# Converting the raw words of a weight piece before its place is free

## The chip, the core and the metric

The kernel runs on one core of a Trainium2 chip. Its engines are TensorE (matmuls into PSUM), VectorE, ScalarE, GpSimd and SyncE (SP, which issues most of the transfers); each works through a queue of its own in order. The metric is the device time of one execution in microseconds, the median over runs. The times vary by about 0.1% from run to run.

## What is computed

Attention over 4 batches of 8 heads with 576 positions and 64 columns, causal by blocks of 64; then a gated layer on 2304 tokens of 512 columns; then a layer of 8 experts of which each token uses two. Cut to what matters:

```python
scores = where(mask, q @ k.T / 8, -1e9)
x = softmax(scores) @ v                      # 32 heads, then (2304, 512)
x = ((x @ w1) * (x @ w2)) @ w3 @ w_out       # w3 (1024, 1024), w_out (1024, 512)
out = sum of the two best experts' weights * (relu(x @ m1[e]) @ m2[e])
```

## The kernel before

**Precision and pieces.** Every float32 operand of a matmul is split into a high part, rounded to the matmul's type (ScalarE, L489), and a low part, the difference (VectorE or GpSimd, L493); a product is three matmuls (L498, L499, L500). The weights of the gated layer arrive as the raw 64-bit words of doubles. They are loaded piece by piece into a raw buffer (`load64`, L554, two buffers, on SP's queue), turned into float32 by three integer instructions on VectorE (`conv64`, L563, L564, L565) in one staging buffer (`stf`, there is only one), and split from there into a place: one of twelve tiles pc0 to pc11, of 2 x 1024 columns.

**The product of the weights.** While the attention of the first heads runs, the kernel also works out w3 @ w_out, once, in 64 units of three matmuls of 512 columns (`w_unit`); eight units make one half of a result tile (pc8 to pc11). w_out lies in pc0 to pc3; the eight slices of w3 pass through pc4 and pc5 in turn. Then the slices of w1 and w2 take pc6, pc7, and pc4, pc5, pc0 to pc3 once the product is done. So most pieces have a place that units still read. The list of jobs has 23 pieces (`w_jobs`), each with its source, its place and the number of units that must have been emitted before the place can be taken over (the last entry, `at`): 16 to 48 for the slices of w3 from the third on, 64 for the last six pieces, else 0.

**The order.** The program is written out as a loop over heads: the pass i emits what ends head i and what starts head i + 1, in the order of a string of steps (FIRST for the first ten passes, LATER behind them): g and s and a and b are units of the attention, `c` is a call of `feed`, `f2.9` a call of `fill`. FIRST has three of each. `feed` splits the piece that was converted in the call before, then converts the next one, if the counter of units allows it, and issues the load of the one after the next. `fill` emits units of the product as long as enough pieces are split (`moe1.conv`), for 2.9 us of matmul time by a number in the code (0.65 a unit), else nothing. When the units are used up, it emits steps of the gated layer.

**What stands in the queues.** The framework then orders each engine's queue at build, by what is ready and by the place of an instruction in the emitted program. Offsets in the code shift that place: pieces count as emitted 60 instructions later (PIECE_PRIO), units of the product 400 later (W_PRIO), the gated layer's matmuls 200 later (MOE_PRIO). So the place of a step in the program is not the time at which it runs, but once built, the order on each engine is fixed.

**Other lines that are named.** L660 and L663 are the matmuls of the scores (tile sb), L674 the reductions that find each row's maximum (negated), L677 joins the two of the last tile of a head (once in a head). L628 to L633 split q and k, L693 transposes the probabilities, L699 splits them from head 8 on, L718 multiplies by v. L196 (GpSimd) and L201 (VectorE) make the first tokens of the gated layer out of eight heads' results: a sum, and a product with the reciprocals of the row sums.

Of the kernel before, what the change touches and what calls it, by code (L numbers as in the profile page):

```python
# [476 lines left out]
class Kernel:  # L477
# [91 lines left out]
    def attention(self):  # L569
# [3 lines left out]
        with tc.tile_pool(name="p1", bufs=1, side="right") as p1, \  # L573
# [162 lines left out]
            wst = {}  # L736
# [18 lines left out]
            def w_jobs():  # L755

                def wout(g):
                    return a["w_out"][:, g:g + 1, :], 1, g // 2, (g % 2) * 512, 0

                def wout2(g):  # L760
                    return a["w_out"][:, g:g + 2, :], 2, g // 2, 0, 0

                def w3(ft, o, w=512):
                    return a["w3"][ft, :, o:o + w].unsqueeze(1), 1, 4 + ft % 2, o, 0 if ft < 2 else max(16, 8 * (ft - 1))

                for half in range(2):
                    for ft in range(2):
                        yield w3(ft, half * 512)
                    if half == 0:
                        for g in range(2):  # L770
                            yield wout(g)
                    for g in range(2 + 2 * half, 4 + 4 * half, 2):
                        yield wout2(g)
                for ft in range(2, 8):
                    yield w3(ft, 0, 1024)
                for m, (n, k, i) in enumerate(W12):
                    yield a[n][:, :, k * 256:(k + 1) * 256], 4, i, 0, 0 if m < 2 else 64

            jobs = list(w_jobs())
            raw = []  # L780

            conv = []

            def feed():

                with tc.high_priority(offset=PIECE_PRIO):
                    feed_half()

            def feed_half():
                if len(conv) > wst.get("split", 0):  # L790
                    _, _, i, o, _ = jobs[len(conv) - 1]
                    pc, w = self.pc[i], conv[-1].shape[-1]
                    self.split((pc[:, 0, o:o + w], pc[:, 1, o:o + w]), conv[-1], low="dve")
                    wst["split"] = len(conv)
                    moe1.conv += w // 512
                n = len(conv)
                if n < len(jobs) and wst.get("n", 0) >= jobs[n][4]:
                    conv.append(self.conv64(raw[n]))
                    if n + 2 < len(jobs):
                        raw.append(self.load64(*jobs[n + 2][:2]))  # L800
# [370 lines left out]
```

## Time and profile before

| | us |
|---|---|
| median of three runs | 1068.72 (1068.28 to 1069.4) |
| the profiled execution, its own time | 1066.87 |
| its span, first to last instruction | 1065.0 |
| TensorE busy in it | 1030.6 (97%) |
| VectorE, ScalarE, GpSimd busy | 558.3, 497.8, 306.5 |

The profile is one execution, 1.85 us faster than the median of the runs. Times inside it count from the start of the span. A busy TensorE is not one at its peak, since matmuls are pipelined and their ends are modelled; an idle one is a loss if it has work that waits. The heads' attention fills the first 440 us, the product of the weights lies in its first 126 us, and the experts' layer ends the kernel.

### The profile page before, as it was taken

How to read it: one execution, taken by the hardware profiler on the slowest of the kernel's cores; microseconds unless marked ns; L12 is line 12 of the kernel's file. 1: busy time of each engine (PE TensorE's matmuls, PEld its weight loads, DVE VectorE, ACT ScalarE, POOL GpSimd, SP SyncE). 2: the span in 40 equal slices, each digit the busy share in tenths (PEclk: the TensorE clock that was granted, in tenths of full speed). 3: DMA queues.
4: the chain of work that ended last, by engine and by line, in shares of the span. 5: the costliest groups of instructions: out<-in, count | busy, mean ns of one | idle time of the engine just before them, and what ended most of it. 6: DMA issues, size and time to landing. Idle time of an engine off the chain costs nothing.

```text
span 1065.0 us, 17408 instructions
## 1 busy us (share of the span) xinstructions
PE 1030.6 (97%) x6612; PEld 932.9 (88%) x6612; DVE 558.3 (52%) x1198; ACT 497.8 (47%) x1176; POOL 306.5 (29%) x309
## 2 busy tenths in 40 slices
PE   6899898999999999999999999999999999999996
PEld 4677697898999999899999889989898989899896
DVE  7987999585755757534245443533333333434110
ACT  6775567565665665523224433533333333334110
POOL 1000334234252425142345134341404132220212
PEclk9999999999999999999999999999999999999998
DMA  8764786437542553222424355763646454351312
GB/s 278 255 229 131 226 243 127 121 111 167 165 115 85 152 181 96 74 87 60 80 61 120 96 126 148 208 178 72 159 99 156 103 149 109 110 119 31 40 20 33
DMA packets 78722, 136.34 MB, mean 128 GB/s; under 512 B 21245, under 2 KB 46053, under 8 KB 77477
## 3 DMA queue, kind: packets, MB, share of 16 engines
q1 hardware_dynamic: 68149, 113.19, 36.5%
q0 software_dynamic: 10480, 21.95, 11.3%
q8 instruction: 54, 0.88, 0.4%
q14 instruction: 39, 0.32, 0.1%
HBM read 103.92 MB, written 31.19 MB: 127 GB/s over the span
## 4 chain that ended last, share of the span: by engine, by line
PE 88%; DVE 8%; ACT 1%; issue 1%; DMA 1%; POOL 0%; SPq 0%; POOLq 0%; DVEq 0%; ACTq 0%
PE ph L498 14%; PE ph L500 14%; PE ph L499 14%; PE m L498 10%; PE m L499 10%; PE m L500 10%; PE av L718 4%; PE tp L693 4%; PE sb L663 2%; PE sb L660 2%; PE m L977 2%; DVE nm L674 1%; DVE stf L564 1%; DVE stf L565 1%; DVE hi L630 1%
## 5 line engine op out<-in xcount | busy, mean ns | idle before, releaser
L498 PE MATMUL m<-xh,pc 128*128 128x256 f32 x576 | 162.2, 286 | 0.6 <-DVE lgs L285 0.3
L499 PE MATMUL m<-xh,pc 128*128 128x256 f32 x576 | 159.8, 282 | 0.0
L500 PE MATMUL m<-xh,pc 128*128 128x256 f32 x576 | 159.2, 282 | 0.0
L499 PE MATMUL ph<-xt,pc 128*128 128x384 f32 (+1 forms) x512 | 156.9, 307 | 0.0
L500 PE MATMUL ph<-xt,pc 128*128 128x384 f32 (+1 forms) x512 | 156.9, 306 | 0.0
L498 PE MATMUL ph<-xt,pc 128*128 128x384 f32 (+1 forms) x512 | 156.3, 307 | 0.0
L994 DVE SCALAR_TENSOR_TENSOR ht<-ph,ht 128x384 fp32r<-128x384 f32 (+1 forms) x128 | 62.2, 490 | 148.1 <-ACT ht L993 148.1
L493 DVE TENSOR_TENSOR pc<-stf,pc 128x1024 fp32r<-128x1024 f32 (+1 forms) x75 | 87.7, 1182 | 88.7 <-ACT pc L489 83.0
L498 PE MATMUL ph<-pc,ht 128*128 128x512 f32 (+1 forms) x328 | 127.9, 390 | 0.0
L1040 POOL DMA_INDIRECT out_dram<-yo,ids x39 | 65.4, 1677 | 213.4 <-ACT yo L1036 98.7
L499 PE MATMUL ph<-pc,ht 128*128 128x512 f32 (+1 forms) x328 | 125.9, 384 | 0.0
L500 PE MATMUL ph<-pc,ht 128*128 128x512 f32 (+1 forms) x328 | 125.9, 385 | 0.0
L993 ACT ACTIVATE ht<-ph 128x384 fp32r<-128x384 f32 (+1 forms) x128 | 55.6, 438 | 132.3 <-PE ph L500 132.0
L679 ACT ACTIVATE pb<-sb,nm 128x288 f32<-128x288 f32 (+3 forms) x192 | 93.8, 498 | 46.3 <-PE tp L693 26.9
L498 PEld LDWEIGHTS m<-xh,pc 128*128 128x128 f32 x576 | 107.9, 189 | 1.4 <-DVE ps L341 0.6
L499 PEld LDWEIGHTS m<-xh,pc 128*128 128x128 f32 x576 | 107.7, 188 | 0.6
L500 PEld LDWEIGHTS m<-xh,pc 128*128 128x128 f32 x576 | 107.1, 188 | 0.3
L493 POOL TENSOR_TENSOR gt<-at,gt 128x256 fp32r<-128x256 f32 x72 | 58.9, 821 | 146.5 <-ACT gt L489 146.3
L489 ACT CAST pc<-stf 128x1024 fp32r<-128x1024 f32 (+1 forms) x75 | 75.0, 1016 | 47.0 <-DMA stf<-in_m_dram 30.1
L499 PEld LDWEIGHTS ph<-xt,pc 128*128 128x128 f32 x512 | 96.1, 188 | 0.3
L498 PEld LDWEIGHTS ph<-xt,pc 128*128 128x128 f32 x512 | 96.1, 188 | 0.4
L500 PEld LDWEIGHTS ph<-xt,pc 128*128 128x128 f32 x512 | 96.2, 188 | 0.0
(162 smaller groups left out, 2170.7 us busy)
## 6 DMA issues: line engine op xcount, KB each, us to landing
stf<-in_m_dram SPq DMA_DIRECT2D x52, 512.0 KB
qk<-in_qk_dram SPq DMA_DIRECT2D x31, 576.0 KB
stg<-in_w_dram SPq DMA_DIRECT2D x14, 1024.0 KB
x<-ev SPq DMA_DIRECT2D x64, 144.0 KB
xab<-x SPq DMA_DIRECT2D x10, 512.0 KB
yt<-y SPq DMA_DIRECT2D x18, 260.0 KB
v<-in_v_dram SPq DMA_DIRECT2D x24, 160.0 KB
out_dram<-cst SPq DMA_DIRECT2D x3, 1280.0 KB
```

Source lines behind the costliest of these rows:

```text
L489: d = nc.scalar.copy(h, src)
L493: return d, eng.tensor_tensor(l, src, r32(h), op=OP.subtract)
L498: nc.tensor.matmul(out, a, c, start=first, stop=False)
L499: nc.tensor.matmul(out, a, d, start=False, stop=False)
L500: nc.tensor.matmul(out, b, c, start=False, stop=last)
L660: nc.tensor.matmul(o, lh, c.hi[:, 1, k0:k0 + w], start=True, stop=False)
L679: nc.scalar.activation(pb[t][:, k0:k0 + src.free_size()], src, AF.Exp, bias=nm, scale=1.0, accum_out=sums[:, h // H, t + n, h % H:h % H + 1])
L693: nc.tensor.transpose(bank[:, n * P:(n + 1) * P], pb[t][:, kt * P:(kt + 1) * P], self.ident)
L718: nc.tensor.matmul(c.av[:, o0:o0 + w], c.vv[:, kt, :], c.pt[:, i, s0:s0 + w], start=(kt == 0 and i == 0), stop=(kt == 4 and i == m - 1))
L993: a = nc.scalar.activation(hh[:, 0, f, :], ph, AF.Relu)
L994: v = nc.vector.scalar_tensor_tensor(hh[:, 1, f, :], ph, 0.0, r32(hh[:, 0, f, :]), op0=OP.max, op1=OP.subtract)
L1040: d = nc.gpsimd.indirect_dma_start(out=self.a["out"], out_offset=self.idx(e, i), in_=yo, in_offset=None, compute_op=OP.add)
```

## The change

The counter of units no longer holds back the conversion of a piece (nor the load that follows it), only its split. A call of `feed` that finds a converted piece whose place is not yet free by the counter does nothing; otherwise it splits that piece and always converts the next one.

```diff
             def feed_half():
                 if len(conv) > wst.get("split", 0):
-                    _, _, i, o, _ = jobs[len(conv) - 1]
+                    _, _, i, o, at = jobs[len(conv) - 1]
+                    if wst.get("n", 0) < at:
+                        return
                     pc, w = self.pc[i], conv[-1].shape[-1]
                     self.split((pc[:, 0, o:o + w], pc[:, 1, o:o + w]), conv[-1], low="dve")
                     wst["split"] = len(conv)
                     moe1.conv += w // 512
                 n = len(conv)
-                if n < len(jobs) and wst.get("n", 0) >= jobs[n][4]:
+                if n < len(jobs):
                     conv.append(self.conv64(raw[n]))
                     if n + 2 < len(jobs):
                         raw.append(self.load64(*jobs[n + 2][:2]))
```

## Rows read from the trace of the kernel before

**Rows 1.** Windows: stretch, length, busy us of each engine (instructions), granted clock, transfers.
```profile
76.00:107.00 31.00, 31.00 (x166) 24.57 (x165) 22.08 (x35) 18.92 (x50) 0.00 (x0) 1.00 0.45 146
126.00:138.00 12.00, 8.66 (x42) 6.70 (x41) 11.94 (x18) 7.91 (x20) 4.40 (x3) 0.72 0.67 225
138.00:166.00 28.00, 27.55 (x222) 25.99 (x221) 27.57 (x40) 19.68 (x54) 11.53 (x8) 1.00 0.79 233
166.00:181.00 15.00, 10.00 (x74) 8.80 (x74) 14.94 (x26) 10.85 (x28) 8.01 (x5) 1.00 0.37 94
181.00:1065.00 884.00, 873.46 (x5695) 804.55 (x5693) 397.93 (x947) 376.95 (x866) 270.88 (x267) 1.00 0.44 110
```

**Rows 2.** The chain of waits up to 260 us: start, length, what.
```profile
85.98 0.46 PE m L498 x2
...
176.92 1.74 DVE stf L565
```

**Rows 3.** Timeline of VectorE: start, length, line, operation, out<-in, count.
```profile
112.54 0.15 DVE L677 TENSOR_REDUCE nm<-nm 128x1 f32<-128x2 f32 x1
...
181.03 1.21 DVE L493 TENSOR_TENSOR pc<-stf,pc 128x1024 fp32r<-128x1024 f32 x1
```

**Rows 4.** Timeline of VectorE around pieces 11 and 12.
```profile
78.35 1.22 DVE L493 TENSOR_TENSOR pc<-stf,pc 128x1024 fp32r<-128x1024 f32 x1
...
80.08 0.68 DVE L563 TENSOR_SCALAR stf<-stg 128x1024 int32<-128x1024 int32 x1
...
82.33 1.22 DVE L565 SCALAR_TENSOR_TENSOR stf<-stg,stf 128x1024 int32<-128x1024 int32 x1
```

**Rows 5.** Window of L500's matmuls alone (units of the product, one each): TensorE, its weight loads.
```profile
0.00:85.00 85.00, 10.84 (x29) 5.46 (x29) 1.00 0.74 240
```

**Rows 6.** Timeline of ScalarE: high halves of pieces 12 and 14.
```profile
90.13 1.05 ACT L489 CAST pc<-stf 128x1024 fp32r<-128x1024 f32 x1
...
106.64 1.05 ACT L489 CAST pc<-stf 128x1024 fp32r<-128x1024 f32 x1 [0.97 <-PE m L499]
```

**Rows 7.** Groups on VectorE, 76 to 107 us, then one of 107 to 181.
```profile
L674 DVE TENSOR_REDUCE nm<-sb 128x1 f32<-128x288 f32 (+4 forms) x14 | 6.0, 456 | 4.6 <-PE sb L663 4.4
...
L564 DVE SCALAR_TENSOR_TENSOR stf<-stg,stf 128x1024 int32<-128x1024 int32 x3 | 3.7, 1223 | 0.1
L565 DVE SCALAR_TENSOR_TENSOR stf<-stg,stf 128x1024 int32<-128x1024 int32 x3 | 3.7, 1219 | 0.0
...
L565 DVE SCALAR_TENSOR_TENSOR stf<-stg,stf 128x1024 int32<-128x1024 int32 x8 | 11.1, 1393 | 0.1
```

**Rows 8.** Waits of SP's queue, 0 to 200 us: us in total, times, longest.
```profile
SPq L554 <- DVE stf L565: 24.7, 10, 4.5
```

**Rows 9.** Timeline of TensorE: first and last of twelve matmuls, and the product's last.
```profile
118.56 0.39 PE L498 MATMUL m<-pc,pc 128*128 128x512 f32 x1
...
121.08 0.39 PE L500 MATMUL m<-pc,pc 128*128 128x512 f32 x1
...
124.89 0.39 PE L500 MATMUL m<-pc,pc 128*128 128x512 f32 x1
```

**Rows 10.** Timeline of TensorE: the first scores of two heads.
```profile
38.33 0.25 PE L660 MATMUL sb<-hi 128*128 128x192 f32 x1
...
44.70 0.49 PE L660 MATMUL sb<-hi 128*128 128x192 f32 x1
```

**Rows 11.** Waits of VectorE, 76 to 107 us.
```profile
DVE nm L674 <- PE sb L663: 4.4, 2, 3.1
```

**Rows 12.** Timelines of GpSimd and VectorE: the first tokens.
```profile
125.61 0.92 POOL L196 TENSOR_TENSOR xab<-xab 128x256 f32<-128x256 f32 x1 [4.14 <-DMA xab<-x]
...
133.03 0.43 DVE L201 TENSOR_TENSOR xr<-xab,xr 128x256 f32<-128x256 f32 x1
```

**Rows 13.** Windows, columns as in rows 1.
```profile
126.00:129.00 3.00, 1.61 (x9) 0.94 (x7) 3.00 (x6) 2.99 (x9) 0.58 (x2) 1.00 0.71 257
...
131.00:137.00 6.00, 5.17 (x22) 4.10 (x22) 5.94 (x10) 4.08 (x11) 1.83 (x2) 0.50 0.87 284
```

## The prediction

> **What bounds the kernel now.** I read the windows of the trace by stage first, then the chain of waits, then the queues of VectorE, ScalarE, TensorE and the load queue around the weight pieces. In the windows [rows 1] the reader is to see three regimes. Until 107 us TensorE is busy without a break (31.00 of 31.00 us in 76 to 107) while VectorE has 31.00 - 22.08 = 8.92 us idle. From 126 to 181 us it is the other way round: VectorE is busy 11.94 of 12, 27.57 of 28 and 14.94 of 15 us, and TensorE loses 3.34 + 0.45 + 5.00 = 8.79 us. After 181 us TensorE has work to the end (873.46 of 884 us). The chain of waits says the same [rows 2]: it runs over matmuls of the weight product near 86 us, and over the conversion of a piece (L565) still at 177 us. So only the first 181 us can be touched by this change, and there the price of a gain is read from VectorE: what it finishes earlier than 181 us lets TensorE fill again earlier, at most the 8.79 us.
>
> **Where the pieces stand.** There are 23 pieces. I number them from 0 in the order of the list of jobs; pieces 9 to 14 are the slices of w3 that reuse two places (pc4, pc5), and 17 to 22 are slices of w1 and w2 that reuse places of the product. Counting the counters through the two order strings by hand, before and after, gives this. Before, five feed calls split a piece and convert nothing, since the next one's place is in use (after pieces 8, 10, 11, 12 and 16). After, three calls do nothing instead (ahead of the splits of 12, 13 and 17). So the conversions and splits of 9 and 10 are emitted one feed call earlier, and those of 11 to 22 two, the conversions of 12, 13 and 17 three; the last split moves from the second feed of the pass i = 7 to the third of i = 6. With three such calls to a pass (one head) that is a third of a head to a whole one.
>
> But emission is not execution. The order string puts the last split before the last scores of head 8. Those scores' minimum runs at 112.54 us and the split at 181.03 us [rows 3]: 68 us after its place in the program. The pieces trail because they share one staging buffer: a conversion needs the split before it done. Look at pieces 11 and 12 [rows 4]: the split of 11 starts at 78.35 us, and the conversion of 12 follows at 80.08 and ends at 82.33 + 1.22 = 83.55 us. Its place (pc5) is read by the units of the product up to the 32nd, and at 85 us 29 of them had run their last matmul [rows 5]; ScalarE's half of its split comes at 90.13 us [rows 6]. **So the conversion already runs while the place is in use**, 10 us before the split. For piece 14, too, what ends ScalarE's wait at 106.64 us is a matmul of the product (L499), not the conversion [rows 6]. What the change asks for is, in time, there already.
>
> **The change part by part.**
> 1. Raw conversions emitted earlier: three instructions each for 14 pieces (9 to 22), none added, none removed. They are already behind the split of the piece before; the single buffer keeps them there. 0 us. If the cover were gone (the conversion really moved by a feed), one piece is 0.68 + 1.22 + 1.22 and 1.22 us for its low half, 4.3 us of VectorE [rows 4, 7].
> 2. The early return in the feed call, which holds back the split alone: a split in time waits for the matmuls, not for the counter [rows 6]. 0 us. No wait is added on an engine, since the counter is Python's, at build time.
> 3. Raw loads, 1 MB each, issued with the conversions on SP's queue: they need one of two raw buffers, and what SP's queue waits for there is the conversion's last instruction, 24.7 us in ten waits [rows 8]. Issued earlier in the program they wait for the same. 0 us; below, at most what the loads of the next head's q and k would be held behind them.
> 4. Units of the product (L498 to L500, 64 units of three matmuls): each one from 16 on is emitted one fill call earlier, because the counter of split pieces that gates them is higher at that call. This is the one thing that can really move on TensorE. Twelve of these matmuls start from 118.56 to 121.08 us, so 0.229 us each, 0.69 a unit, 5.5 us for the eight that free a place [rows 9]. A fill emits up to five units, 3.4 us. But a unit is emitted with an offset of 400 instructions behind the attention's, so it mostly fills holes that the attention leaves, and being emitted one fill earlier changes its turn only where it competes. Lower bound: nothing moves, 0 us. Upper bound: every unit comes 3.4 us earlier. Then pieces 11 to 14 follow 3.4 us earlier, which brings 3.4 / 5.5 x 4.3 = 2.7 us of VectorE work into the idle 8.92 us; but the heads make way by 3.4 us of 6.4 (the same matmul of two heads with no unit between, 38.33 and 44.70 us [rows 10]), and with them go 3.4 / 6.4 x 2.6 = 1.4 us of their score reductions (14 reductions are 6.0 us, six to a head [rows 7]). Net -1.3 us. I take -0.5 us, nearer to nothing, since the rows show fillers.
>
> The last instruction of a conversion, L565, is dearer late: 1219 ns in 76 to 107 us, where GpSimd does nothing, and 1393 ns in 107 to 181 [rows 1, 7]. A piece that slid from the later stretch into the earlier would save 0.17 us there, too little to enter the sum. The Trainium skill's page "SBUF — State Buffer", section "Who interferes with whom", says that VectorE and GpSimd share one port pair as an exclusive lock, which speaks for moving conversions to where GpSimd is quiet; the rows agree in direction, and by the rule too the sum changes by some 0.2 us a piece.
>
> **The sum.** The profiled execution took 1066.87 us (span 1065.0 and 1.87 around it); 1066.87 - 0.5 = 1066.4. That execution is 1.85 us under the median of the runs shown (1068.72), so as a median I forecast 1068.72 - 0.5 = 1068.2 us.
>
> **The rivals.** What one of these runs can tell from no change is about 0.2%, 2.1 us.
>
> A, the forecast: the early emission meets the single staging buffer, and only a few units change their turn. 1068.2 us, own range 1066.7 to 1070.3. For it speaks the early conversion [rows 3 to 6]. Against it: every queue's order is fixed at build, so one unit taken earlier deals the order behind it anew; A needs that this comes out even.
>
> B, faster: the units win their turns, the places come free earlier, and one whole piece (4.3 us) fits into VectorE's idle time before 107 us, which is mostly waiting for score matmuls that stand behind other work in TensorE's queue (4.4 us of it [rows 11]). The crowded stretch then ends near 176.7 instead of 181 us, the loss of TensorE there falls from 8.79 to about 4.5 us, and the time is 1068.72 - 4.3 = 1064.4 us. For it: the gap is twice as long as a piece, and the pieces behind 14 are one chain. Against it: heads pushed back leave a gap of their own.
>
> C, slower: the units are used up earlier while the attention and the first tokens of the next layer come no earlier. The units are what fills TensorE until 124.89 us [rows 9]. The tokens' sum is ready at 126.5 us, and the product with the reciprocals waits in VectorE's queue until 133.03 us [rows 12], so a head 7 that is up to 6.5 us later costs nothing there, and an earlier end of the units gains nothing. TensorE is then without filler from 121.5 us. By the idle share of the hole (3.34 of 12 us [rows 1]) that is 3.4 x 0.28 = 0.95 us more. The hole also has a price in clock: TensorE was busy 1.61 of the 3 us from 126 to 129 us, and from 131 to 137 us the granted clock is 0.50, the lower level of 1.2 GHz, with 5.17 of 6 us of matmuls in it [rows 13]. 3.4 us more at half the pace with matmuls in 0.86 of it lose 1.46 us. 1068.72 + 2.4 = 1071.1 us. It decides where the last unit ends before 122 us and VectorE's crowd does not end sooner. The Trainium skill's page "TensorE: Matmul & The Clock Gate", section "What's actually happening", says that "the default state is throttled, and activity releases the throttle"; by that rule a longer hole is paid at the lower clock, and this trace agrees with its 0.50.
>
> **How the numbers follow.** A 0.46, B 0.30, C 0.24. A is likeliest since the conversions already run in front of their splits; B is above C because the idle time of VectorE that it uses is there, and C's loss partly hides behind a VectorE that is full anyway. The range for 8 in 10 reaches to both: 1064.3 to 1071.4 us. Faster by over 0.2%: 0.30; within: 0.46; slower: 0.24.
>
> **What would show it.** In the profile after: the conversions (L564, L565) of the pieces again right behind the split of the piece before, the last low half near 181 us (A), at 177 or earlier (B), or no earlier with TensorE's busy time in 126 to 138 below 8.66 us (C). The last matmul of the product starts at 124.89 us now; 121 to 122 us would say that the units won their turns. TensorE's loss from 126 to 181 us, 8.79 us now, should differ by what the time differs. I am wrong if VectorE's idle time in 76 to 107 us shrinks by more than 2 us, or if the order of the two load kinds on SP's queue changes so that a head waits for its q and k.

## The result, and the profile after

| | before | after |
|---|---|---|
| median, us (runs) | 1069.4 (5: 1068.28 to 1070.8) | 1077.3 (5: 1073.57 to 1079.34) |
| ratio of the runs | | 1.0074, interval [1.0058, 1.0089] |
| the profiled execution, us; its span | 1066.87; 1065.0 | 1079.34; 1077.5 |

The change makes the kernel slower by 7.9 us. The forecast (1068.2, range 1064.3 to 1071.4) is wrong, and so is its sign. The two profiled executions lie farther apart than the medians, by 12.5 us: the one after is the slowest of its five, and the one before is faster than all five.

The windows of the kernel after, in the columns of [rows 1]:

```profile
76.00:107.00 31.00, 31.00 (x168) 24.93 (x168) 21.73 (x36) 19.24 (x50) 0.00 (x0) 1.00 0.45 149
...
126.00:138.00 12.00, 7.36 (x37) 5.44 (x37) 11.94 (x18) 8.39 (x23) 3.35 (x3) 0.77 0.72 208
138.00:166.00 28.00, 27.32 (x198) 25.56 (x198) 25.09 (x37) 16.48 (x47) 8.02 (x6) 0.92 0.89 247
166.00:181.00 15.00, 11.21 (x81) 9.31 (x79) 14.54 (x20) 9.42 (x27) 8.18 (x5) 1.00 0.25 72
...
255.00:300.00 45.00, 41.71 (x302) 38.16 (x301) 29.36 (x88) 26.80 (x78) 14.50 (x16) 0.96 0.54 168
440.00:480.00 40.00, 38.57 (x292) 35.98 (x291) 24.98 (x80) 21.09 (x61) 11.04 (x12) 0.96 0.18 52
```

and of the kernel before, the last two stretches, which were not shown yet:

```profile
255.00:300.00 45.00, 44.66 (x329) 40.46 (x329) 32.57 (x90) 30.56 (x89) 17.38 (x18) 1.00 0.62 167
...
440.00:480.00 40.00, 39.70 (x295) 37.06 (x294) 16.62 (x61) 13.28 (x35) 13.01 (x14) 1.00 0.23 66
```

Up to 107 us little differs from [rows 1]; VectorE's idle time there is 31 - 21.73 = 9.27 us, where it was 8.92. From 126 to 181 us TensorE loses 4.64 + 0.68 + 3.79 = 9.11 us, where it was 8.79; what differs there is the clock, 0.77 and 0.92 instead of 0.72 and 1.00, and what the engine does: by the groups of lines it runs the same 56 x 3 matmuls of the gated layer, but only 20 pairs of scores (L660, L663) where there were 24, 34 products by v where there were 39. And there are holes where there were none: 3.29 us from 255 to 300 (0.34 before) and 1.43 from 440 to 480 us (0.30 before).

The timeline of VectorE after, for piece 12 and the last piece, and of TensorE, for the product's last matmul and the two holes near 260 us (in brackets: idle time before, and what ended it):

```profile
79.50 1.22 DVE L493 TENSOR_TENSOR pc<-stf,pc 128x1024 fp32r<-128x1024 f32 x1
...
81.23 0.68 DVE L563 TENSOR_SCALAR stf<-stg 128x1024 int32<-128x1024 int32 x1
...
181.92 1.21 DVE L493 TENSOR_TENSOR pc<-stf,pc 128x1024 fp32r<-128x1024 f32 x1
```

```profile
125.25 0.40 PE L500 MATMUL m<-pc,pc 128*128 128x512 f32 x1
...
260.50 0.35 PE L660 MATMUL sb<-hi 128*128 128x192 f32 x1 [1.46 <-DVE hi L630]
270.67 0.55 PE L693 MATMUL tp<-ident,pb 128*128 128x128 f32 x3 [1.83 <-DVE ev L708]
```

No piece came earlier: the conversion follows the split of the piece before as in [rows 4], the last split starts at 181.92 us (181.03 in [rows 3]), the last unit at 125.25 (124.89 in [rows 9]). What came later is the attention. The last head starts (L628) at 449.5 us, before at 424.1.

The chain of waits after, behind 240 us, shows what that costs first (start, length, what):

```profile
240.60 7.80 DMA x<-ev
...
250.04 0.29 SPq L733
250.38 3.55 DMA rs<-st
...
254.67 3.57 DMA xr<-rs
...
258.36 1.24 DVE xr L201
```

and VectorE's timeline, what stands behind it:

```profile
253.34 0.46 DVE L674 TENSOR_REDUCE nm<-sb 128x1 f32<-128x288 f32 x1
258.36 1.23 DVE L201 TENSOR_TENSOR xr<-xab,xr 128x1024 f32<-128x1024 f32 x1 [4.56 <-DMA xr<-rs]
259.51 0.15 DVE L677 TENSOR_REDUCE nm<-nm 128x1 f32<-128x2 f32 x1
259.69 0.76 DVE L630 SCALAR_TENSOR_TENSOR hi<-qk,hi 64x576 fp32r<-64x576 f32 x1
```

The third chunk of tokens needs the row sums of the second batch. They are made at 246.4 us now (L730; 236.03 before), go to memory (L733) and come back (L166, at 254.00 us; 240.50 before). The store waits until 250.04 us, since on SP's queue a load of tokens stands ahead of it, which waits for the transfer x<-ev of 7.80 us. The product with the row sums (L201) stands in VectorE's queue at its fixed place, waits 4.56 us, and the attention's own small steps (L677, L630) stand behind it, so TensorE waits for the low half of q. Before, their load was issued 15 us ahead of that product, there was no wait, and L630 stood in front. (The second hole, at 270.67 us, has another cause: L708 waits 1.67 us for a transfer, x<-ev.) VectorE before:

```profile
255.06 0.76 DVE L630 SCALAR_TENSOR_TENSOR hi<-qk,hi 64x576 fp32r<-64x576 f32 x1
255.85 2.38 DVE L201 TENSOR_TENSOR xr<-xab,xr 128x1024 f32<-128x1024 f32 x1
```

**An account of the time.** For each profiled execution I took windows of 5 us over the whole span and summed TensorE's idle time, and its busy time times (1 - granted clock). The span less both is what is left; it is 1027.7 us before, 1029.9 after, and 1028.0 to 1032.3 in all runs below. So the kernels differ in the main by their holes and by the half clock (1.2 GHz) that stands behind many of these: before 34.4 and 2.9 us, after 38.9 and 8.7. That is 10.3 of the 12.5 us between the two executions; the other 2.2 us stay unexplained.

### The profile page after: what moved, and what is told of

It is laid out like the page before. It is cut to its first block, busy times and chain, and to the rows that moved or that the text cites. A ratio compares the mean times of both kernels' runs of the same rounds, so it can differ in the third digit from the quotient of the medians.

```text
span 1077.5 us, 17413 instructions
## 1 busy us (share of the span) xinstructions
PE 1038.6 (96%) x6612; PEld 937.9 (87%) x6612; DVE 558.1 (52%) x1198; ACT 497.0 (46%) x1176; POOL 303.9 (28%) x309
## 4 chain that ended last, share of the span: by engine, by line
PE 85%; DMA 6%; DVE 5%; ACT 2%; issue 1%; SPq 1%; POOL 0%; POOLq 0%; DVEq 0%; ACTq 0%
PE ph L498 14%; PE ph L500 14%; PE ph L499 14%; PE m L498 9%; PE m L499 9%; PE m L500 9%; PE av L718 4%; PE tp L693 4%; DMA x<-ev 2%; PE sb L663 2%; PE sb L660 2%; DMA stg<-in_w_dram 2%; PE m L979 2%; DMA rs<-st 1%; PE m L255 1%; DVE nm L674 1%
## 5 line engine op out<-in xcount | busy, mean ns | idle before, releaser
L500 PE MATMUL m<-xh,pc 128*128 128x256 f32 x576 | 160.0, 284 | 1.2 <-DVE pc L493 1.2
L500 PE MATMUL ph<-xt,pc 128*128 128x384 f32 (+1 forms) x512 | 156.9, 306 | 0.0
L500 PE MATMUL ph<-pc,ht 128*128 128x512 f32 (+1 forms) x328 | 125.9, 385 | 0.0
L500 PEld LDWEIGHTS m<-xh,pc 128*128 128x128 f32 x576 | 107.9, 190 | 1.9 <-DVE pc L493 1.7
L493 POOL TENSOR_TENSOR gt<-at,gt 128x256 fp32r<-128x256 f32 x72 | 61.7, 860 | 161.2 <-ACT gt L489 161.0
L674 DVE TENSOR_REDUCE nm<-sb 128x1 f32<-128x128 f32 (+2 forms) x192 | 79.0, 437 | 37.3 <-PE sb L663 37.0
L489 ACT CAST pc<-stf 128x1024 fp32r<-128x1024 f32 (+1 forms) x75 | 74.9, 1017 | 46.7 <-DMA stf<-in_m_dram 28.5
L499 PEld LDWEIGHTS ph<-xt,pc 128*128 128x128 f32 x512 | 96.1, 188 | 0.3
L498 PEld LDWEIGHTS ph<-xt,pc 128*128 128x128 f32 x512 | 96.1, 188 | 0.4
```

What stands on the lines that cost most here:

```text
L489: d = nc.scalar.copy(h, src)
L493: return d, eng.tensor_tensor(l, src, r32(h), op=OP.subtract)
L498: nc.tensor.matmul(out, a, c, start=first, stop=False)
L499: nc.tensor.matmul(out, a, d, start=False, stop=False)
L500: nc.tensor.matmul(out, b, c, start=False, stop=last)
L674: nc.vector.tensor_reduce(nm[:, n:n + 1], o[:, 0:w], axis=AX, op=OP.max, negate=True)
```

## The experiments

Each ratio is to the kernel before in runs made beside it on the same chip; e1 to e4, e5 to e8, e9 to e12 and e13 to e16 ran together. "Last head" is the start of the last L628; "hole 260" is idle plus clock loss from 255 to 300 us, "420" the same from 300 to 440.

| run | median, us | ratio to before | idle, clock, us | last head | hole 260 | 420 |
|---|---|---|---|---|---|---|
| before | 1069.4 | | 34.4, 2.9 | 424.1 | 0.3 | 0.2 |
| after | 1077.3 | 1.0074 [1.0058, 1.0089] | 38.9, 8.7 | 449.5 | 4.8 | 0.0 |
| e1 | 1070.76 | 1.0001 [0.9985, 1.0016] | 34.1, 5.6 | 426.7 | 0.3 | 0.2 |
| e2 (after, as built) | 1083.37 | 1.0103 [1.0082, 1.0123] | 39.9, 8.9 | 448.9 | 4.0 | 0.5 |
| e3 | 1082.95 | 1.0100 [1.0079, 1.0121] | 39.4, 10.5 | 428.5 | 1.3 | 5.9 |
| e4 | 1095.95 | 1.0225 [1.0197, 1.0252] | 46.7, 15.1 | 463.7 | 11.2 | 5.3 |
| e5 (after) | 1083.64 | 1.0110 [1.0085, 1.0135] | 42.0, 10.2 | 454.7 | 3.6 | 6.5 |
| e6 | 1086.34 | 1.0132 [1.0102, 1.0163] | 41.0, 11.4 | 456.4 | 5.0 | 6.7 |
| e7 | 1070.92 | 0.9995 [0.9981, 1.0009] | 35.0, 6.0 | 427.4 | 0.6 | 0.2 |
| e8 | 1085.7 | 1.0119 [1.0091, 1.0146] | 44.5, 7.7 | 427.5 | 0.3 | 4.7 |
| e9 (after) | 1078.31 | 1.0072 [1.0051, 1.0092] | 38.7, 10.1 | 450.3 | 4.6 | 0.4 |
| e10 | 1074.2 | 1.0054 [1.0031, 1.0077] | 37.4, 3.8 | 443.7 | 0.6 | 0.0 |
| e11 | 1075.2 | 1.0058 [1.0039, 1.0077] | 37.9, 5.6 | 447.3 | 4.1 | 0.0 |
| e12 | 1072.39 | 1.0022 [1.0011, 1.0033] | 35.5, 6.0 | 438.3 | 0.1 | 0.8 |
| e13 | 1072.98 | 1.0038 [1.0026, 1.0049] | 33.7, 8.8 | 445.8 | 0.4 | 0.3 |
| e14 | 1075.49 | 1.0056 [1.0040, 1.0072] | 35.4, 7.6 | 426.7 | 0.5 | 0.1 |
| e15 | 1076.99 | 1.0071 [1.0055, 1.0086] | 36.4, 7.5 | 441.8 | 0.2 | 0.8 |
| e16 | 1070.21 | 1.0013 [1.0000, 1.0027] | 33.5, 5.6 | 431.2 | 0.1 | 0.5 |

### Which part of the change does it (e1, e2)

```diff
+    v = wst.get("v", 0)              # counters as in the kernel before
+    if v > wst.get("vs", 0): wst["vs"] = v; wst["vconv"] = ...
+    if v < len(jobs) and wst.get("n", 0) >= jobs[v][4]: wst["v"] = v + 1
...
-                    while moe1.conv < need:
+                    while wst.get("vconv", 0) < need:      # e1
+                    while (moe1.conv if n < 25 else wst.get("vconv", 0)) < need:      # e2
```

> The change without its effect on the units: pieces are converted, loaded and split at the feed calls of the changed kernel, and the units of the product wait for the calls at which the kernel before emitted them (a second set of counters keeps those calls). Theory O (the change acts only through the units, whose earlier emission deals TensorE's order anew): nothing moves, 1069 us, within 2 us of the kernel before, the last head's split of q (L628) at 424 us as before. Rival L (loads and conversions that are emitted earlier stand ahead of q, k and the first tokens on the load queue): most of the 8 us stays, 1074 us or more, and the last tokens of eight heads land near 127 us instead of 122.7.

> As the run before, but units 16 to 24 of the product, nine of 48, go at the fill calls of the changed kernel; units 25 to 63 keep the calls of the kernel before. Theory O: the first turn that changes deals all that follows, so nine units do what 48 do: 1077 us, the last head's L628 near 449 us. Rival U (each unit that is used up earlier leaves TensorE without filler for its own time, so the loss goes with their number): 9/48 of 8 us, 1.5 us, 1070.5 us.

e1 converts, loads and splits without the old bound and only keeps the units where they were: 1.0001. By the code, its conversions come one or two calls earlier than in the kernel before and its splits one; the changed kernel has its splits up to two earlier, since its units, which free the places, come earlier too. Each queue of e1, as built, holds the rows of the kernel before in the same order. So three of the four parts of the change do nothing by themselves, and rival L falls in its simple form.

e2 does not do what was expected of it. It was to move units 16 to 24 alone, but the counters that hold units 25 to 63 count the units emitted so far (`n`), and these now come earlier. By the code, all 48 units then go at the calls of the changed kernel, and as built the order of each queue is that of the changed kernel, row for row. So e2 is the changed kernel once more, at 1.0103. Whether nine units do what 48 do was not tested, nor was rival U by number. What e1 shows beside the changed kernel is that the whole effect comes in with the units' calls.

### The place of the attention (e3, e4)

```diff
-FIRST = "g0 g1 t f2.9 ... f2.9 c t a f2.9 ..."
+FIRST = "g0 g1 t f3.3 ... f3.3 c t a f3.3 ..."
```

> The changed kernel with fills of 3.3 us instead of 2.9 in the first ten passes, so that the units are emitted earlier still; no work is added. Its order puts the attention about as far ahead of the gated layer's matmuls as the kernel before has it. Theory O (what costs is that the attention falls a head behind, and the gated layer then waits for it near 260 and 450 us): 1069 us, within 3 us of the kernel before, last L628 at 420 to 430 us, no hole of over 1 us in TensorE near 260 us. Rival U (units used up earlier cost by themselves): 1077 us or more.

> The kernel before, without the change, with the same 3.3 us. Its order puts the attention about as far behind as in the changed kernel. Theory O: 1077 us, 1074 to 1080, last L628 near 450 us, waits near 260 and 450 us. Rival L or U (it is the change's loads, conversions or units): the change isn't there and the fill is 0.4 us longer, at most 2 us, 1069 to 1071 us. Rival N (the place of the attention says nothing, any new order is worth some us either way): e3 and e4 do not stand on opposite sides.

Theory O took the loss for a matter of one thing, how far the attention stands behind the gated layer. e4 is on the expected side (last head 463.7 us, 11.2 us lost near 260), though far beyond 1077. e3 is not: its attention is ahead, the hole near 260 us is small, and it is 1.0% slower all the same. It loses 5.9 us near 430 us instead, at a place explained under e5. Theory O falls as the only cause, and rival N's sign is there: the two don't stand on opposite sides. e3 alone would suit rival U (1077 us or more), but e4 doesn't, where U and L had 1069 to 1071. What holds is the account by holes, which e3 fits (the span less its holes and clock is 1030.7 us).

### The wait near 260 us (e6, e7, e9, e10)

e6 and e7 (the third chunk's product on GpSimd), then e10 (the store of the second batch's row sums from ScalarE's queue):

```diff
-    d = nc.vector.tensor_tensor(x.r[:, g:e, :], ...
+    d = (nc.gpsimd if c == 2 else nc.vector).tensor_tensor(x.r[:, g:e, :], ...
```

```diff
-    nc.sync.dma_start(self.rs[b][:, ...
+    (nc.scalar if b == 1 else nc.sync).dma_start(self.rs[b][:, ...
```

> The changed kernel once more, to stand beside the others on the same chip. Expected 1.006 to 1.010 of the kernel before, with the holes of TensorE near 133, 260 and 270 us and near 450 us again, since the order of each queue is fixed.

> The changed kernel, but the product with the reciprocals (L201) of the third chunk of tokens, the one that waits 4.56 us in VectorE's queue for the row sums at 258 us, is done by GpSimd; the order of the other queues hardly moves. Theory H (TensorE's work is the same in all kernels, about 1037 us, and the time is that and its holes, each with a stretch at half clock behind it; the holes near 260 and 270 us come from L201's wait in VectorE's queue): 3.3 us of holes and 1.7 us of clock go, 4 to 5 us less than the changed kernel in the same job. Rival Q (the attention is late by itself, and VectorE's wait only shows it): the holes stay near 255 to 280 us or come up behind, within 1.5 us of the changed kernel.

> The kernel before with the same one instruction moved, as a control. There the row sums are loaded at 240.5 us, long before that product (255.85 us), and VectorE doesn't wait. Theory H: nothing to gain, within 2 us of the kernel before. If moving the instruction is worth something by itself (2.4 us less on VectorE), it shows here as a gain too.

> The changed kernel, the base for the two runs beside it. Expected 1.007 to 1.011 of the kernel before: at the lower end where the low half of q (L630) near 420 us starts before GpSimd's four operations and takes about 1 us, at the upper where it starts behind them and takes 5.5 us.

> The changed kernel with the reciprocal row sums of the second batch stored from ScalarE's queue, since on SP's the store stands behind a load of tokens from 247.34 to 250.04 us; five transfers change their queue and little else moves. Theory H2 (the hole near 260 us is the wait of L201 in VectorE's queue, whatever holds its data back): the row sums come 2.7 us earlier, the wait of 4.56 us falls to about 2, and the hole of 1.5 to 2 us before the scores near 260 us goes; 1.5 to 3 us less than the changed kernel beside it. Rival Q (the attention is late and the hole stays wherever the wait goes, as with the product on GpSimd): no less.

e6 missed: nothing came back. Its trace says why, GpSimd's queue first, then TensorE's:

```profile
257.86 2.36 POOL L201 TENSOR_TENSOR xr<-xab,xr 128x1024 f32<-128x1024 f32 x1 [2.37 <-DMA xr<-rs]
260.18 1.40 POOL L633 TENSOR_TENSOR kl<-qk,hi 128x576 fp32r<-128x576 f32 x1
```

```profile
261.64 0.43 PE L663 MATMUL sb<-kl,hi 128*128 128x192 f32 x1 [2.61 <-POOL kl L633]
```

The same late data now hold up GpSimd, and behind it the low half of k instead of that of q: the wait was moved, not removed. e7, the control, shows that the edit itself is worth nothing where no wait is (0.9995).

e10 makes the data earlier. The window of 255 to 300 us in e9 (the changed kernel, run beside it) and VectorE in it:

```profile
255.00:300.00 45.00, 41.74 (x300) 37.88 (x300) 30.72 (x88) 26.34 (x79) 14.88 (x16) 0.96 0.55 168
```

```profile
258.86 1.23 DVE L201 TENSOR_TENSOR xr<-xab,xr 128x1024 f32<-128x1024 f32 x1 [5.37 <-DMA xr<-rs]
260.00 0.15 DVE L677 TENSOR_REDUCE nm<-nm 128x1 f32<-128x2 f32 x1
260.19 0.75 DVE L630 SCALAR_TENSOR_TENSOR hi<-qk,hi 64x576 fp32r<-64x576 f32 x1
```

and the same in e10:

```profile
255.00:300.00 45.00, 44.44 (x336) 40.81 (x335) 33.59 (x94) 28.25 (x82) 21.52 (x19) 1.00 0.61 161
```

```profile
253.22 2.96 DVE L630 SCALAR_TENSOR_TENSOR hi<-qk,hi 64x576 fp32r<-64x576 f32 x1
256.21 2.32 DVE L201 TENSOR_TENSOR xr<-xab,xr 128x1024 f32<-128x1024 f32 x1
```

The wait is gone, and L630 now stands ahead of L201. TensorE runs 336 matmuls in this stretch instead of 300, at full clock; the loss there falls from 4.6 to 0.6 us, the median by 4.1 us (1.5 to 3 were expected), the ratio from 1.0072 to 1.0054. The intervals of the two ratios overlap, so the profile carries this more than the times do. By the profile rival Q falls.

Two things changed at once in e10, the time of the data and the place of L630, and e10 doesn't separate them. Two kernels without the change speak for the place. In e15 L201 waits too, but behind L630:

```profile
256.13 1.93 DVE L630 SCALAR_TENSOR_TENSOR hi<-qk,hi 64x576 fp32r<-64x576 f32 x1
...
260.61 1.23 DVE L201 TENSOR_TENSOR xr<-xab,xr 128x1024 f32<-128x1024 f32 x1 [2.55 <-DMA x<-ev]
```

and its hole near 260 us is 0.2 us. In e4 L201 stands ahead of L708 and L630 and waits 7.89 us, and TensorE waits 3.88 us for L708. So the wait alone isn't the hole; it becomes one where the attention's steps stand behind it.

### The raw loads on another queue (e8)

```diff
-            self.nc.sync.dma_start(t.rearrange("p (a b) -> p a b", a=n), src)
+            self.nc.gpsimd.dma_start(t.rearrange("p (a b) -> p a b", a=n), src)
```

> The changed kernel with the raw loads of the pieces issued from GpSimd's queue instead of SP's, so that no load of q, k or tokens stands behind a raw load that waits for its buffer. Rival L (the load queue holds the attention back): the loss goes, 1069 us or less, with q and k of head 11 loaded before 150 us. Theory H: another order with holes of its own; the time is 1037 us and its idle and clock losses, on either side of the changed kernel, and L alone explains nothing if the loss near 255 to 275 us stays.

After the change, q and k of head 12 (counted from 0; the expectation calls it 11) stand on SP's queue behind two raw loads (before: behind the first of them), and are issued at 156.09 us, before at 148.34. SP's queue, and what VectorE runs just ahead of that load:

```profile
142.24 9.99 SPq L554 DMA_DIRECT2D stg<-in_w_dram  x2
156.09 0.35 SPq L611 DMA_DIRECT2D qk<-in_qk_dram  x1
```

```profile
154.07 1.96 DVE L630 SCALAR_TENSOR_TENSOR hi<-qk,hi 64x576 fp32r<-64x576 f32 x1
```

The raw loads are issued by 152.2 us. What the load then waits for, 3.8 us, is L630 of the head before, which reads the same buffer and ends at 156.03 us. So its delay is that of the attention, not of the raw loads. In e8 no raw load stands in front; q and k of heads 12 and 13 go at 140.56 and 154.94 us, the attention is ahead (last head 427.5 us), the hole near 260 is gone, and the kernel is 1.2% slower. The edit deals the whole order anew, so it doesn't say what the old order with free loads would take; but free loads are not enough to win back the 8 us.

### VectorE held by GpSimd (e5, e11, e13)

The changed kernel itself stands at 1.0110 in e5, just above what was expected, and at 1.0074 and 1.0072 the two other times, with the same order. The profile of e5 has a hole near 424 us that the two others lack. GpSimd, VectorE and TensorE in e5:

```profile
418.86 0.75 POOL L493 TENSOR_TENSOR gt<-at,gt 128x256 fp32r<-128x256 f32 x1
419.56 2.37 POOL L196 TENSOR_TENSOR xab<-xab 128x1024 f32<-128x1024 f32 x1
421.90 1.39 POOL L633 TENSOR_TENSOR kl<-qk,hi 128x576 fp32r<-128x576 f32 x1
423.25 0.85 POOL L641 TENSOR_TENSOR vv<-v,vv 128x320 fp32r<-128x320 f32 x1
```

```profile
419.08 5.64 DVE L630 SCALAR_TENSOR_TENSOR hi<-qk,hi 64x576 fp32r<-64x576 f32 x1
```

```profile
424.87 0.50 PE L660 MATMUL sb<-hi 128*128 128x192 f32 x1 [3.29 <-DVE hi L630]
```

and the same two engines in the first profile after the change:

```profile
419.73 1.30 POOL L493 TENSOR_TENSOR gt<-at,gt 128x256 fp32r<-128x256 f32 x1
421.01 2.39 POOL L196 TENSOR_TENSOR xab<-xab 128x1024 f32<-128x1024 f32 x1
```

```profile
419.32 1.12 DVE L630 SCALAR_TENSOR_TENSOR hi<-qk,hi 64x576 fp32r<-64x576 f32 x1
```

L630 takes 0.76 us when left alone. In e5 it began 0.22 us after GpSimd's first operation, GpSimd ran four without a gap, and L630 ended at 424.72 us, 0.62 us after the last of them. In the first profile it began 0.41 us ahead of that operation; it took 1.12 us, and GpSimd's took 1.30 instead of 0.75. So with a shift of 0.6 us come 3.3 us of hole and 2.9 us of clock. The hole of e3 near 430 us is of this kind too (an L630 of 5.45 us). The collision isn't all that sets the runs of one program apart: e2, the same program at 1.0103, has none in its profile (0.5 us lost from 300 to 440).

e11 takes the longest of the four operations away from GpSimd; e13 has this and the edit of e10:

```diff
-    d = nc.gpsimd.tensor_tensor(x.ab[:, g:e, 0, :], ...
+    d = (nc.vector if c == 5 else nc.gpsimd).tensor_tensor(x.ab[:, g:e, 0, :], ...
```

> The changed kernel, but the sum of the sixth chunk of tokens (L196, 2.39 us on GpSimd near 420 us) is done by VectorE. Theory K (GpSimd's run of operations without a gap keeps VectorE's L630 from running): L630 of that head takes under 2.5 us and the hole of 3.3 us in TensorE near 420 us goes with the half clock behind it, 4 to 6 us less than the changed kernel wherever that has the collision, and the runs lie closer together. Rival (L630 is slow for another reason, as a late operand): L630 takes over 4 us again.

> The changed kernel with both edits of the runs before: row sums stored from ScalarE's queue and the sixth chunk's sum on VectorE. If the two losses are separate (wait of L201 near 260 us; VectorE's L630 held by GpSimd near 420 us, where it happens), they add: 1.003 of the kernel before, 1.001 to 1.005; the rest is what the later attention costs at 126 to 181 us and behind 440 us. If one wait only stands in for the other, 1.005 as the one edit alone.

e11 is inconclusive on theory K: the changed kernel beside it (e9) had no such collision in its profile (0.4 us lost from 300 to 440), so there was nothing to remove, and its 1.0058 is not told apart from 1.0072. e13 stands at 1.0038 [1.0026, 1.0049], as forecast and just below the changed kernel's intervals: the two edits together give back about half of the loss. Their shares aren't told apart, since the interval overlaps that of e10 alone. The other half stays; of what the profile shows, 0.9 us lie at the end of the attention near 445 us, and the rest in part at 126 to 181 us (13.8 us of idle and clock in e13, 11.6 before, 12.1 and 11.5 in e1 and e7, which have the order of before there).

### Other deals of the order (e12, e14, e15, e16)

Four kernels without the change, in which the same work is only counted or emitted at another place:

```diff
-PIECE_PRIO, W_PRIO, MOE_PRIO = -60, -400, -200
+PIECE_PRIO, W_PRIO, MOE_PRIO = -60, -250, -200      # e12
+PIECE_PRIO, W_PRIO, MOE_PRIO = -60, -400, -100      # e16
...
-LATER = "... f2.6 ... f2.6 ... f2.6 ..."
+LATER = "... f2.9 ... f2.9 ... f2.9 ..."            # e14
...
-                    while moe1.conv < need:
+                    while moe1.conv < need + (n % 8 > 3 and 16 <= n < 56):      # e15
```

> The kernel before, without the change, with the units of the product counted 250 instructions late instead of 400: nothing is added or taken away, only TensorE's order is dealt anew from about 85 us on. Theory D (the change is one deal of the order among many, and the order before happens to be a good one): slower by 0.3 to 1.5%, with holes in VectorE's waits again. Rival (the order of the change is a bad one in its own right, through its earlier units): 1069 to 1072 us, within 0.2% of the kernel before.

> The kernel before with fills of 2.9 us instead of 2.6 in the passes behind the tenth: no work added, TensorE's order is as before up to about 190 us and dealt anew behind it, with the attention as far ahead as before or farther. Theory H (the loss comes where the attention falls behind the gated layer): no hole near 260 us, within 0.3% of the kernel before. Rival (any new deal costs 0.5 to 1%, wherever the attention stands): 1074 to 1080 us.

> The kernel before with half of the units of the product held back until the next slice of w3 is split, so that they come later and not earlier; no work added. In its order the attention stands some 30 matmuls farther back than before from 200 us on, as in the changed kernel. Theory H: slower by 0.3 to 1%, with the wait of L201 for the row sums near 260 us again. Rival U (it is the earlier units): later units cost nothing or gain, 1066 to 1070 us.

> The kernel before with the gated layer's matmuls counted 100 instructions late instead of 200: the order is as before up to about 230 us, then the attention falls back a little, by up to 18 matmuls near 400 us. Theory H: no wait near 260 us, a part of the loss behind 440 us at most: 0 to 0.4% slower.

Three are slower, by 0.22 to 0.71%; e16, whose order is that of before up to about 220 us, by 0.13%, at the edge of what can be told. e15 holds units back instead of emitting them early and costs as much as the change (1.0071), so rival U falls in its other form. But theory H isn't saved by it: e15 has no hole near 260 us (its loss is 6.2 us from 181 to 255, 0.4 before), and e14, with the attention as far ahead as before, is at 1.0056 with 3.9 us lost from 440 to 480; there H, which had 0.3% at most, missed, and its rival (any new deal costs 0.5 to 1%) did not. e12 came just under the 0.3 to 1.5% that were expected. Each order has holes of its own at other places. No kernel that was run is measurably faster than the kernel before. Whether the order before had been chosen for its time is not on record; if it had, new orders would be slower for that reason alone.

## Why the prediction was wrong

**Parts 1 to 3 (conversions, early return, raw loads: 0 us): right.** e1 has all three and measures 1.0001. The reason given, the single staging buffer, agrees with the traces: the queues as built don't change at all.

**Part 4 (units): the right part, the wrong size and sign.** It was named as the one thing that can really move, and e1 shows that nothing else does. But it was costed at -0.5 us, between 0 and -1.3, from the units' own time (3.4 us of filler). The units hardly moved: the last starts 0.36 us later, not earlier.

**The step that failed** is the sentence "So only the first 181 us can be touched by this change." It bounded every case. Units that change their turn, from 85.6 us on in the traces, dealt anew what stands behind them on all engines, for over 350 us: the attention fell 25 us behind (last head), and in-order queues met waits that had been covered. Of the 10.3 us that the two profiles differ in holes and clock, 4.5 lie from 255 to 300 us (4.8 less 0.3) and 2.6 from 440 to 480 (2.9 less 0.3), outside of the bound. TensorE's idle time from 126 to 181 us, which was to differ by what the time differs, grew by 0.32 us.

**A reading.** That TensorE is busy without a break until 107 us holds for 76 to 107 us; of the first 76 us it is busy 60.92. No term of the sum rests on it.

**Rival A** named its own condition, that the new deal "comes out even". It didn't, and in seven other deals tried here (e3, e4, e8, e12, e14, e15, e16) it never came out as a gain. No row spoke for an even deal, on which the chance of 0.46 rests.

**Rival B (faster)** failed at its first step: no piece came earlier, and VectorE's idle time before 107 us grew by 0.35 us instead of shrinking by 4.3.

**Rival C (slower)** had the sign, not the mechanism. Its test, TensorE's busy time in 126 to 138 us below 8.66, came true (7.36), but the units were not used up earlier (125.25 us, not 121 to 122), so its 2.4 us is not what was measured.

**The other warning**, an order of the two load kinds in which a head waits for its q and k, came true in its first half only: a raw load did move ahead of those of head 12, but their load waited for L630 (3.8 us) and not for it.

**What stays open:** about half of the loss, 0.3 to 0.4%, goes with the edits of e10 and e13. The profiles put it near 260 us (4.6 us in e9, 0.4 in e13); that the collision near 420 us has a share in the median is argued from e5 and not shown, since no run took away one that the kernel beside it had. For the rest the profiles show where TensorE is idle or at half clock, but no edit took it away. Why the first changed turn puts the attention back and not forward was not found out, nor how few units would do it; it is settled when the order is built.

## What to carry to other kernels

Where a framework orders the queues at build, first find out whether a change alters that order at all. If it doesn't, the change is worth nothing (e1); if it does, the work that moved is no measure of the effect, and the price lies in waits at the heads of in-order queues, perhaps hundreds of us later. Look for what stands behind such a wait: the stretch lost 4.8 us where L630 stood behind it, and 0.2 us where L630 stood in front (e15). An earlier store took it away here, with L630 in front as well (e10); handing it to another engine's queue only moved it (e6). Seven other orders of this kernel's work were 0.1 to 2.3% slower and none faster, so a case in which the order of such a kernel is dealt anew deserves a large chance of being slower. And read from the queues as built whether a control differs from the kernel as meant: e2 did not.

## What the hardware showed that was not expected

**One engine can keep another out for a run of instructions.** L630 (0.76 us) took 5.64, 5.45, 5.47 and 5.49 us in e5, e3, e4 and e6, as long as GpSimd went on without a gap. Of the 576 L630 in all traces, the 166 that had no GpSimd operation beside them took 0.75 to 0.76 us, and these four are the only ones over 3 us, which speaks against a late operand as the reason. The Trainium skill's page "SBUF — State Buffer", section "SBUF: two separate sides", says of a VectorE operation with two inputs in SBUF and a GpSimd operation that reads SBUF that whichever starts first gets the shared ports for the whole instruction and the other blocks. The trace agrees for the first instruction; that VectorE didn't get its turn between GpSimd's four is seen here only in the rows. And it isn't always so. In e10 L630 began at 253.22 us, just behind L196 on GpSimd, and ended at 256.18, so it got in ahead of L633, which took 1.93 us instead of 1.39:

```profile
253.17 2.40 POOL L196 TENSOR_TENSOR xab<-xab 128x1024 f32<-128x1024 f32 x1
255.53 1.93 POOL L633 TENSOR_TENSOR kl<-qk,hi 128x576 fp32r<-128x576 f32 x1
```

What decides between the two was not found out.

**The same hole is not always followed by half clock.** Windows of 1 us before and after, where both have a hole of 1.85 us that ends at 48.71 and 49.29 us:

```profile
51.00:52.00 1.00, 1.00 (x6) 0.83 (x5) 1.00 (x2) 0.81 (x3) 0.00 (x0) 1.00 1.03 426
52.00:53.00 1.00, 1.00 (x6) 0.84 (x5) 1.00 (x3) 0.20 (x1) 0.00 (x0) 1.00 0.93 372
```

```profile
51.00:52.00 1.00, 1.00 (x5) 0.75 (x4) 1.00 (x3) 0.90 (x3) 0.00 (x0) 0.50 0.94 369
52.00:53.00 1.00, 1.00 (x4) 0.76 (x4) 1.00 (x2) 0.59 (x3) 0.00 (x0) 0.50 0.99 390
```

The order of TensorE's queue is the same up to there. After it ran at 0.50 (1.2 GHz) and lost 1.7 us; before at 1.00. e10 and e13, which have one order up to about 400 us, differ in the same way (0 and 1.7 us lost up to 126 us). So a part of the spread between executions is the clock's answer to holes that are always there.
